# Group scores called ahead of the step's copies, 22 and 11 portions, the fourth MM1 block in a half tile, and two small VectorE operations in place of GpSimd's

## The chip, the cores and the metric

The kernel runs on one core of a Trainium2 chip. A core has five engines, each with an instruction queue of its own that it works off in order: TensorE (PE, with PEld for its weight loads), VectorE (DVE), ScalarE (ACT), GpSimd (POOL) and SyncE (SP, which here only issues transfers). Engines wait for one another through semaphores. The metric is the device time of one execution in microseconds.

## What is computed

Attention with one more term in the denominator, then a feed-forward layer with a Mish activation. The part that matters:

```python
q, k, v: (batch 8, heads 12, seq 448, head_dim 64), float32
w_in: (768, 2048), w_out: (2048, 768)

def _attn_ref(q, k, v):
    scores = scale * np.matmul(q, k.transpose(0, 1, 3, 2))
    m = np.max(scores, axis=-1, keepdims=True)
    e = np.exp(scores - m)
    attn = e / (np.sum(e, axis=-1, keepdims=True) + np.exp(-m) + 1e-09)
    return np.matmul(attn, v)

def _moe_ref(x, w_in, w_out):      # x: (batch * seq, heads * head_dim)
    h = x @ w_in
    sp = np.where(h > 20.0, h, np.log1p(np.exp(np.minimum(h, 20.0))))
    g = h * np.tanh(sp)
    return g @ w_out
```

## The kernel before

**Tiling.** Two heads make a pair, six pairs a batch (`HP`), 48 pairs in all. A pair takes four steps: in each, PE computes scores (L350 to L366) into a score tile, VectorE takes the negated row maxima (L369, `negm`), and ScalarE the exponentials with their sums (L387, into `en`). There are three score tiles in PSUM, `sc_tiles`, each of two halves of 512 float32 columns, used in turn: the scores of step i + 3 need the exponentials of step i done. Two single PSUM tiles, `mo_tiles`, serve everything else; they are handed out in the order in which they came back (`mo_take`, `mo_free`).

After a pair's last step VectorE forms the denominators and their reciprocals (`denominators`, L404 and L408). For most pairs of the first two batches the division comes later, as a multiplication of the outputs: the reciprocals are split into two bf16 parts, hi and lo (`hl`, L412 and L413), which PE spreads over the rows of a PSUM tile by 16 small matmuls (`spread_rden`, L432). The exponentials are transposed by a DMA (`normalise`, L462, `en` to `eT`), for a few pairs on PE (`turn_on_pe`). The product with v (`av_pair`, L497) follows some pairs later and gives `xT`.

**Units.** The first loop works on the six pairs 0 to 5 (`HEAD` is 6), the rest goes in units of three pairs, that is twelve steps (u from 2). After a unit's steps come eight blocks of the first matrix product (MM1: `mm1_mish`, `mm1`, six L556 matmuls each), each followed by ScalarE's Mish (L572) from PSUM into `gT`; blocks belong to the batch before. From u = 4 on the second product (MM2: `mm2_part`, L616, 16 matmuls for a portion of output columns) is spread over a unit's attention steps as a filler: a list of twelve weights says what share of it goes to which step. From u = 6 to 15 units are "grouped": the pairs' steps are mixed, the weights are `weight_paired`, and after steps 0, 2 and 4 no scores are written, so that two steps' scores come together after steps 1, 3 and 5 (`GROUP_AT`). Within a step the order of the calls is: exponentials, pending copies (`flush_late`), the filler's portions, scores.

**The order** of each engine's instructions is that of the calls: the program is scheduled by hand. Waits are put in by the framework, which follows what each instruction reads and writes tile by tile; where two instructions touch different halves of one tile, the code can declare them independent (`apart`, L237), and does so in attention at some places.

**Block banks.** `mm1_bank(ff, ahead)` puts the third block of a unit (index 2) into the first half of `sc_tiles[0]`, and if `ahead` is 2 the fourth block (index 3) into its second half; all others take a single tile. Before, `ahead` is 2 only for the blocks of the first batch (units 2 and 3), the first four of which in attention steps are begun early (`mm1_begin`).

**GpSimd's queue at the sixth pair.** In the first loop `load_w(n, behind=p-1)` makes GpSimd copy two elements of pair p-1's `eT` into `marks` (L172), which waits until that transfer has landed, then issue n weight transfers (L177); the reciprocals' parts and the casts of q, k and v (L194) stand behind these in its queue. The parts of pair 5, the sixth, are read by PE in unit 2, at step 5 (`RDEN_AT`).

Of the kernel before, what the change touches and what calls it, by code (L numbers as in the profile page):

```python
# [12 lines left out]
ALU = mybir.AluOpType  # L13
# [6 lines left out]
def kernel(  # L20
# [9 lines left out]
    nc = tc.nc  # L30
# [88 lines left out]
    def flush_late():  # L119
        while late:  # L120
            late.popleft()()
# [5 lines left out]
    def mo_take():  # L127

        if not mo_free:
            flush_late()  # L130
        return mo_free.popleft()
# [104 lines left out]
    def apart(later, *earlier):  # L236

        for e in earlier:
            tc.declare_no_dep(later.ins, e.ins, reason="they read different PSUM banks")
# [51 lines left out]
    def pair_step(idx):  # L291
        if idx < mixed_from:
            return divmod(idx, STEPS)
        u, at = divmod(idx, UNIT_PAIRS * STEPS)
        pi, s = MIXED[at]
        return u * UNIT_PAIRS + pi, s
# [24 lines left out]
    def scores_ahead(limit):  # L321

        n = max(0, min(limit - rg["next"], len(sc_tiles) - rg["used"]))
        for _ in range(n):
            rg["used"] += 1
            scores(rg["next"], paired=n > 1)
            rg["next"] += 1
# [48 lines left out]
    def exps(idx):  # L376
        p, s = pair_step(idx)
        if p >= N_PAIRS:
            return
        st = att[p]  # L380
        sc, cols = st.pop(("sc", s))
        rg["used"] -= 1
        if s == STEPS - 1 and p >= HP and p % UNIT_PAIRS == UNIT_PAIRS - 1:
            w = st["whole"]
            nc.scalar.activation(out=w["expm"], in_=w["negm"], func=AF.Exp)
        for bk, c in enumerate(cols):
            e = nc.scalar.activation(  # L387
                out=st["en"][:, :, c, 0:SP_],
                in_=sc[:, bk, 0:S].rearrange("q (j c) -> q j c", j=NT),
                func=AF.Exp, bias=st["negm"][:, c : c + 1], scale=1.0,  # L390
                accum_out=st["sums"][:, c : c + 1],
            )
            if idx in av_read:
                apart(e, av_read.pop(idx))
            if idx in av_beside:
                apart(e, *av_beside.pop(idx))
            if s == STEPS - 1:
                half_exp[p] = e
        if s == STEPS - 1 and p < HP:
            nc.scalar.activation(out=st["expm"], in_=st["negm"], func=AF.Exp)  # L400

    def denominators(p, n=1):
        st = att[p] if n == 1 else att[p]["whole"]
        nc.vector.scalar_tensor_tensor(  # L404
            out=st["den"], in0=st["sums"], scalar=1e-9, in1=st["expm"],
            op0=ALU.add, op1=ALU.add,
        )
        nc.vector.reciprocal(out=st["rden"], in_=st["den"])  # L408
        if p < LATE_DIV:
            hl = hl_pool.tile([128, 2, UNIT_PAIRS, NTILE], BF16, tag="hl", name="hl")  # L410
            hi, lo = (hl[:, x, 0, :] if n == 1 else hl[:, x, 0:n, :] for x in range(2))
            nc.gpsimd.tensor_copy(out=hi, in_=st["rden"])  # L412
            nc.gpsimd.tensor_tensor(out=lo, in0=st["rden"], in1=hi, op=ALU.subtract)  # L413
            for i in range(n):
                att[p + i]["hl"] = hl[:, :, i, :]

# [50 lines left out]
    def turn_on_pe(p, j, busy_first=0):  # L467

        st = att[p]
        own = mo_take()  # L470
        keep_busy(busy_first, bank=own)
        ps = own[:, :].bitcast(BF16).rearrange("c (i q) -> c i q", q=128)
        for i in range(NTILE):
            nc.tensor.transpose(ps[0:SP_, i, :], st["en"][:, j, i, 0:SP_], ident)

        def evac():
            nc.vector.tensor_copy(  # L477
                out=st["eT"][0:SP_, j, :].rearrange("c (i q) -> c i q", q=128),
                in_=ps[0:SP_, 0:NTILE, :],
            )  # L480
            mo_free.append(own)

        late.append(evac)
# [66 lines left out]
    def mm1_bank(ff, ahead=2):  # L550
        at = ff % FF_U - 2
        return sc_tiles[0][:, at, :] if 0 <= at < ahead else mo_take()

    def mm1(b, ff, bank, lo, hi):
        for dm in range(lo, hi):
            nc.tensor.matmul(  # L556
                bank[:, 0:S],
                lhsT=w_in_sb[:, dm, ff * 128 : (ff + 1) * 128],
                rhs=xT[b][:, dm, :],
                start=(dm == 0), stop=(dm == DM_T - 1),  # L560
            )

    def mm1_mish(b, ff):
        flush_late()
        at = ff % FF_U - 2
        spare = 0 <= at < (2 if b == 0 else 1)
        if (b, ff) in begun:
            h_ps, lo = begun.pop((b, ff))
        else:
            h_ps, lo = mm1_bank(ff, 2 if b == 0 else 1), 0  # L570
        mm1(b, ff, h_ps, lo, DM_T)
        nc.scalar.activation(out=gT[:, ff, b % 2 * S : b % 2 * S + S], in_=h_ps[:, 0:S], func=AF.Mish)  # L572
        if not spare:
            mo_free.append(h_ps)
# [79 lines left out]
    PAIRED_FROM = first_mm2 + 2  # L654
    GROUP_AT, AV_AT_STEP = (1, 3, 5), 8
    Q_AT = (0, 6, 7)
    weight_paired = [21, 0, 12, 0, 12, 0, 5, 6, 0, 0, 0, 0]

    LEAD = UNIT_PAIRS + 1
    LOAD_AT = (0, 3, 6)  # L660
# [1 line left out]
    HEAD = HP  # L662
# [26 lines left out]
    for p in range(HEAD):  # L689
        for s in range(STEPS):  # L690
# [11 lines left out]
            if s == 0:  # L702
                transpose_pair(p + 2)
                if p:
                    denominators(p - 1)
# [14 lines left out]
            if s < 3:  # L720
                keep_busy(2, half=p)
    denominators(HEAD - 1)

    for u in range(UNITS_PER_B, N_UNITS + 2 * UNITS_PER_B):
# [6 lines left out]
        grouped = attn and u >= PAIRED_FROM  # L731
# [5 lines left out]
        end = min(nxt, N_PAIRS) * STEPS  # L737

        for n in range(steps):
            defer[0] = attn and u > first_mm2 and nxt < N_PAIRS  # L740
            pi, s = divmod(n, STEPS)
            p, idx = p0 + pi, p0 * STEPS + n
            late_tp = u == UNITS_PER_B and n == STEPS
            exps(idx)
            if u == UNITS_PER_B + 1 and n == 0:
                for j in range(2):
                    turn_on_pe(HEAD, j, busy_first=3)
# [16 lines left out]
            if grouped and n == AV_AT_STEP:  # L764
# [1 line left out]
                    av_pair(p0 + i - UNIT_PAIRS, half=p0 + i)  # L766
                flush_late()
                av_pair(p0 - 1, act=True)
            if not grouped or n + 1 not in GROUP_AT:
                scores_ahead(end)  # L770
            if n in LOAD_AT and u <= first_mm2:
                at = p0 + LOAD_AT.index(n)
# [8 lines left out]
            elif n == 0 and u <= N_UNITS:  # L781
                nc.gpsimd.tensor_copy(  # L782
                    out=marks[0:1, 5, 0:2], in_=att[p0 - 1]["en"][0:1, NT - 1, NTILE - 1, 0:2]
# [12 lines left out]
            if (u, n) in MORE_LOADS:  # L796
                at = MORE_LOADS[u, n]
# [38 lines left out]
        b, w = (u - UNITS_PER_B) // UNITS_PER_B, u % UNITS_PER_B  # L836
# [3 lines left out]
        for f in range(FF_U):  # L840
            if moe:
                mm1_mish(b, w * FF_U + f)
            if u == UNITS_PER_B and f == 3:
                load_w(5, behind=p0 + 2)
            if u == first_mm2 - 1 and f == FF_U - 1:
                load_w(4, behind=p0 + 1)
            if not attn:
                continue
            if f == 0:
                denominators(p0, UNIT_PAIRS)  # L850
                for p in todo[:first]:
                    normalise(p, dma=p not in BY_PE)
            if f in (1, 3, 5):
                if nxt < BY_DMA_FROM:
                    transpose_pair(nxt + f // 2, bank=f // 2 % 2)
                    evac_qk(nxt + f // 2)
            if f == 1 and p0 < LATE_DIV:
                for p in todo[first:]:
                    normalise(p, dma=p not in BY_PE)
            if f == FF_U - 1:  # L860
                scores_ahead(min(nxt * STEPS + len(sc_tiles), N_PAIRS * STEPS))
            third = 5 if nxt >= BY_DMA_FROM else FF_U - 1
            if f in (3, third) and p0 >= LATE_DIV:
                p = todo[1 + f // 5]
                normalise(p, dma=p not in BY_PE)
# [32 lines left out]
```

## Time and profile before

| | us |
|---|---|
| median of three runs | 459.73 |
| lowest and highest | 454.26 and 459.82 |
| the profiled execution | 459.73 |
| its span in the profile | 457.9 |

| share of the span on the chain that ended last | |
|---|---|
| PE | 72% |
| ACT | 10% |
| DVE | 6% |
| issue (nothing that the profile shows was waited for) | 6% |
| DMA | 3% |
| POOL | 2% |

How to read the rows below. A row of a timeline is: start, length, engine, line of the kernel, operation, what it writes and reads, shapes, and the count, if several of the same kind run one after the other; in brackets how long the engine had been idle before, and what ended that. Matmuls overlap, so 0.36 us for one is its latency, and a row of many shows the rate. In a row of windows stand the window, its length, the busy times of PE, PEld, DVE, ACT and POOL with counts, the clock that TensorE was granted (1.00 is full), the mean busy share of the 16 DMA engines, and GB/s.

### The profile page before, as it was taken

The page shows a single profiled execution, that of the slowest core. Times are in us where ns is not written, and L with a number is a line of the kernel's source. Part 1 is how long each engine was busy: PE and PEld are TensorE (multiplying, and loading weights), DVE is VectorE, ACT ScalarE, POOL GpSimd, SP SyncE. Part 2 cuts the span into 40 slices and gives each one's busy share as a digit, 9 for nine tenths or more (in the row PEclk, how much of TensorE's full clock was granted, in tenths as well). Part 3 has the DMA queues.
Part 4 walks back from the last instruction along what each step waited for, and adds up shares of the span by engine and source line. Part 5 has one row for each costly group of instructions (what it writes and reads, how often), then busy time and mean ns, then how long its engine had stood idle before and what let it go on. Part 6 is the DMA issues. An engine that isn't in the chain of part 4 may idle for free.

```text
span 457.9 us, 8637 instructions
## 1 busy us (share of the span) xinstructions
PE 436.2 (95%) x2991; PEld 232.1 (51%) x2991; DVE 327.3 (71%) x666; ACT 335.8 (73%) x884; POOL 138.6 (30%) x269
## 2 busy tenths in 40 slices
PE   7878699999999999999999999999999999999996
PEld 3334355445555545545454545554554555556565
DVE  5999678888797868778787878786878878311021
ACT  5999578989787969798887979796979788221300
POOL 4442638316054233232424242413233210100000
PEclk9999899999999999999999999999999999999999
DMA  8999999999999999999999999999999793920213
GB/s 233 260 209 162 246 227 212 264 235 207 242 238 273 237 279 241 250 230 283 236 257 236 259 253 229 266 214 273 229 245 252 205 243 106 246 65 2 69 36 103
DMA packets 232652, 97.93 MB, mean 214 GB/s; under 512 B 189344, under 2 KB 229152, under 8 KB 232608
## 3 DMA queue, kind: packets, MB, share of 16 engines
q1 hardware_dynamic: 225088, 91.07, 86.9%
q0 software_dynamic: 7488, 6.29, 9.3%
q8 instruction: 23, 0.38, 0.4%
q14 instruction: 21, 0.17, 0.1%
q10 hardware_dynamic: 32, 0.01, 0.0%
HBM read 45.61 MB, written 11.01 MB: 124 GB/s over the span
## 4 chain that ended last, share of the span: by engine, by line
PE 72%; ACT 10%; DVE 6%; issue 6%; DMA 3%; POOL 2%; DVEq 0%; ACTq 0%; POOLq 0%
PE mo L556 27%; PE mo L616 24%; ACT en L387 7%; PE sc L497 5%; PE sc L356 4%; PE sc L556 4%; DVE negm L369 4%; DMA eT<-en 3%; PE sc L350 2%; PE mo L497 2%; ACT L387 2%; POOL w_in_sb L177 1%; DVE o_sb L601 1%; PE sc L309 1%; DVE eT L477 1%
## 5 line engine op out<-in xcount | busy, mean ns | idle before, releaser
L387 ACT ACTIVATE en<-sc,negm 128x448 bf16<-128x448 f32 x336 | 208.9, 640 | 12.4 <-DVE negm L369 11.7
L369 DVE TENSOR_REDUCE negm<-sc 128x2 f32<-128x896 f32 x192 | 179.4, 970 | 48.5 <-PE sc L359 36.1
L616 PE MATMUL mo<-w_out_sb,gT 128*128 128x384 bf16 (+1 forms) x1040 | 159.1, 304 | 0.0
L556 PE MATMUL mo<-xT,w_in_sb 128*128 128x448 bf16 x660 | 131.7, 353 | 0.9 <-DVE xT L517 0.3
L616 PEld LDWEIGHTS <-gT 128*128 128x128 bf16 x1040 | 93.9, 98 | 60.8 <-issue 13.9
L556 PEld LDWEIGHTS <-w_in_sb 128*128 128x128 bf16 x768 | 74.3, 98 | 70.9 <-issue 5.1
L572 ACT ACTIVATE gT<-mo 128x448 bf16<-128x448 f32 x110 | 58.3, 544 | 67.9 <-PE mo L556 67.7
L387 ACT ACTIVATION_READ_ACCUMULATOR en<-sc,negm 128x1 f32 x336 | 71.0, 211 | 0.0
L454 DVE TENSOR_SCALAR en<-en,rden 128x448 bf16<-128x448 bf16 x280 | 70.6, 331 | 0.6
L601 DVE COPY o_sb<-mo 128x192 f32<-128x192 f32 (+1 forms) x65 | 32.4, 498 | 50.2 <-PE mo L616 49.0
L273 POOL TENSOR_SCALAR qd<-qT_all 64x448 bf16<-64x448 bf16 x60 | 33.6, 560 | 89.2 <-DMA qT_all<-q_cast 49.3
L356 PE MATMUL sc<-kT_all,qd 64*128 64x448 bf16 x132 | 42.0, 363 | 2.7 <-ACT en L387 1.3
L359 PE MATMUL sc<-kT_all,qd 64*128 64x448 bf16 x132 | 42.5, 367 | 0.0
L782 POOL COPY marks<-en 1x2 bf16<-1x2 bf16 x12 | 2.1, 174 | 105.6 <-DVE en L454 105.6
L194 POOL CAST q_cast<-q_f 112x512 bf16<-112x512 f32 x47 | 28.9, 614 | 5.8 <-DMA q_f<-in_q_dram 5.8
L497 PEld LDWEIGHTS <-v_bf 112*64 112x64 bf16 x384 | 19.8, 110 | 20.8 <-issue 10.4
L497 PE MATMUL sc<-eT,v_bf 112*64 112x448 bf16 x256 | 29.2, 364 | 0.4 <-DMA eT<-en 0.4
L194 POOL CAST k_cast<-k_f 112x512 bf16<-112x512 f32 x47 | 28.8, 612 | 1.5 <-DMA k_f<-in_k_dram 1.4
L194 POOL CAST v_bf<-v_f 112x512 bf16<-112x512 f32 x48 | 28.2, 607 | 2.4 <-DMA v_f<-in_v_dram 2.4
L556 PE MATMUL sc<-xT,w_in_sb 128*128 128x448 bf16 x108 | 23.2, 353 | 0.0
L356 PEld LDWEIGHTS <-qd 64*128 64x128 bf16 x132 | 9.1, 95 | 26.7 <-issue 17.9
L350 PE MATMUL sc<-kT_all,qd 128*128 128x448 bf16 x60 | 19.2, 353 | 1.3 <-ACT en L387 1.1
(64 smaller groups left out, 267.8 us busy)
## 6 DMA issues: line engine op xcount, KB each, us to landing
k_f<-in_k_dram SPq DMA_DIRECT2D x48, 224.0 KB, 5.2
q_f<-in_q_dram SPq DMA_DIRECT2D x48, 224.0 KB, 5.3
v_f<-in_v_dram SPq DMA_DIRECT2D x48, 224.0 KB, 5.8
w_in_sb<-in_moe_w_in_dram POOLq DMA_DIRECT2D x12, 256.0 KB, 7.3
w_out_sb<-in_moe_w_out_dram POOLq DMA_DIRECT2D x8, 384.0 KB, 12.2
out_dram<-o_sb SPq DMA_DIRECT2D x7, 336.0 KB, 3.3
out_dram<-o_sb SPq DMA_DIRECT2D x8, 288.0 KB, 3.5
out_dram<-o_sb SPq DMA_DIRECT2D x8, 240.0 KB, 3.0
```

Of the source, the lines that this page charges most:

```text
L194: nc.gpsimd.tensor_copy(out=to[nm], in_=src)
L273: q_reads.append(by.tensor_scalar(out=qd[rows, h * S : (h + 1) * S], in0=q_ps[rows, 0:S], scalar1=SCALE, scalar2=1.0, op0=ALU.mult, op1=AL ...
L356: nc.tensor.matmul(sc[:, 0, 0:S], lhsT=qT[0:64, qa : qa + 128], rhs=kA, start=True, stop=True)
L359: nc.tensor.matmul(sc[:, 1, 0:S], lhsT=qT[64:128, qb : qb + 128], rhs=kB, start=True, stop=True)
L369: half_max[p] = nc.vector.tensor_reduce(out=negm, in_=sc[:, 0 : len(cols), 0:S], axis=AX.X, op=ALU.max, negate=True)
L387: e = nc.scalar.activation(out=st["en"][:, :, c, 0:SP_], in_=sc[:, bk, 0:S].rearrange("q (j c) -> q j c", j=NT), func=AF.Exp, bias=st["neg ...
L454: nc.vector.tensor_scalar(out=en[:, :, i, 0:SP_], in0=en[:, :, i, 0:SP_], scalar1=st["rden"][:, i : i + 1], scalar2=None, op0=ALU.mult,)
L497: mm = nc.tensor.matmul(av[h * 64 : (h + 1) * 64, 0:S], lhsT=v_bf[:, h, j * D : (j + 1) * D], rhs=e_h, start=(j == 0), stop=(j == NT - 1),)
L556: nc.tensor.matmul(bank[:, 0:S], lhsT=w_in_sb[:, dm, ff * 128 : (ff + 1) * 128], rhs=xT[b][:, dm, :], start=(dm == 0), stop=(dm == DM_T - 1),)
L572: nc.scalar.activation(out=gT[:, ff, b % 2 * S : b % 2 * S + S], in_=h_ps[:, 0:S], func=AF.Mish)
L601: nc.vector.tensor_copy(out=o_sb[:, cols], in_=st["o"][:, 0:n_cols])
L616: nc.tensor.matmul(st["o"][:, 0:n_cols], lhsT=gT[:, ff, i * 128 : (i + 1) * 128], rhs=w_out_sb[:, ff, cols], start=(ff == 0), stop=(ff == ...
```

## The change

Four edits. The hi and lo parts of the sixth pair's reciprocals are made by VectorE instead of GpSimd. The fourth MM1 block goes into the second half of the first score tile in all batches, not only in the first. The weights of steps 0 and 2 in grouped units are 22 and 11 instead of 21 and 12; their sum stays 56. In grouped units the scores of steps 1, 3 and 5 are called right after the exponentials, ahead of pending copies and the filler's portions.

```diff
@@ -409,8 +409,9 @@
         if p < LATE_DIV:
             hl = hl_pool.tile([128, 2, UNIT_PAIRS, NTILE], BF16, tag="hl", name="hl")
             hi, lo = (hl[:, x, 0, :] if n == 1 else hl[:, x, 0:n, :] for x in range(2))
-            nc.gpsimd.tensor_copy(out=hi, in_=st["rden"])
-            nc.gpsimd.tensor_tensor(out=lo, in0=st["rden"], in1=hi, op=ALU.subtract)
+            by = nc.vector if p == HEAD - 1 else nc.gpsimd
+            by.tensor_copy(out=hi, in_=st["rden"])
+            by.tensor_tensor(out=lo, in0=st["rden"], in1=hi, op=ALU.subtract)
@@ -563,11 +564,11 @@
     def mm1_mish(b, ff):
         flush_late()
         at = ff % FF_U - 2
-        spare = 0 <= at < (2 if b == 0 else 1)
+        spare = 0 <= at < 2
         if (b, ff) in begun:
             h_ps, lo = begun.pop((b, ff))
         else:
-            h_ps, lo = mm1_bank(ff, 2 if b == 0 else 1), 0
+            h_ps, lo = mm1_bank(ff), 0
@@ -654,7 +655,7 @@
-    weight_paired = [21, 0, 12, 0, 12, 0, 5, 6, 0, 0, 0, 0]
+    weight_paired = [22, 0, 11, 0, 12, 0, 5, 6, 0, 0, 0, 0]
@@ -742,6 +743,8 @@
             exps(idx)
+            if grouped and n in GROUP_AT:
+                scores_ahead(end)
             if u == UNITS_PER_B + 1 and n == 0:
@@ -766,7 +769,7 @@
-            if not grouped or n + 1 not in GROUP_AT:
+            if not grouped or (n not in GROUP_AT and n + 1 not in GROUP_AT):
                 scores_ahead(end)
```

## The prediction

> **What bounds the kernel now.** I read the page first, then the busy time by windows, then the order of events at the three places that the diff touches.
>
> ```profile
> span 457.9 us, 8637 instructions
> ## 1 busy us (share of the span) xinstructions
> PE 436.2 (95%) x2991; PEld 232.1 (51%) x2991; DVE 327.3 (71%) x666; ACT 335.8 (73%) x884; POOL 138.6 (30%) x269
> ```
> ```profile
> 40.00:80.00 40.00, 34.56 (x332) 19.59 (x333) 30.77 (x58) 30.62 (x83) 22.47 (x42) 0.96 1.17 225
> 54.70:58.10 3.40, 3.40 (x21) 1.27 (x18) 1.41 (x2) 1.77 (x5) 3.40 (x7) 0.50 1.23 206
> 200.00:250.00 50.00, 49.65 (x318) 25.67 (x318) 39.95 (x83) 42.01 (x111) 17.01 (x32) 1.00 1.10 247
> ```
>
> In the steady part (200 to 250 us; the columns are length, then busy time of PE, PEld, DVE, ACT and POOL, granted clock, DMA share, GB/s) PE works 49.65 of 50.00 us at full clock. PE takes its instructions in order, so whatever makes it wait there adds to the time, unless a later wait shrinks by as much. From 40 to 80 us PE is busy for 34.56 of 40.00 us only, the mean clock is 0.96 and the DMA share 1.17: that stretch has slack on PE and none on the transfers. The profiled run took 459.73 us, 1.83 us more than its span; it is also the median of the three runs, so I add to 457.9 and put 1.83 us on top.
>
> **Part 1, the fourth MM1 block in a half tile.** In units 4 to 17 (14 of them, one per unit) the six matmuls of the fourth block go to the second half of the first score tile instead of one of the two single tiles. The instructions, their number and their order stay. What changes is what the first of them waits for. Here is that place in one grouped unit (PE's L556, ScalarE's Mish L572).
>
> ```profile
> 163.47 1.30 PE L556 MATMUL sc<-xT,w_in_sb 128*128 128x448 bf16 x6
> ...
> 164.20 0.98 ACT L572 ACTIVATE gT<-mo 128x448 bf16<-128x448 f32 x2
> 164.80 1.67 PE L556 MATMUL mo<-xT,w_in_sb 128*128 128x448 bf16 x8
> ...
> 165.06 0.55 ACT L572 ACTIVATE gT<-sc 128x448 bf16<-128x448 f32 x1
> ```
>
> The third block (into the half tile) starts at 163.47, and the fourth at 164.80. Eight matmuls in 1.67 us, the last of 0.36 (the length that single matmuls show at 199.53 below), are one per 0.187 us, so PE was free at 163.47 + 6 x 0.187 = 164.59 and waited 0.21 us. It waited for the first block's Mish, which gives its tile back: the two Mish from 164.20 take 0.98, one is 0.54 long, so the first ends at 164.74 and the matmul starts 0.06 later. After the change no single tile has to come free. But a wait is kept by whole tiles, the third block's Mish reads the first half of the very tile whose second half the fourth block writes, and the code declares no independence between the two. The waits of the changed program, which can be read without running it, say so: in all 14 units the first matmul of block four waits for the ScalarE count that the Mish of the third block brings. That Mish runs from 165.06 to 165.61; the fourth block starts at 165.67 instead of 164.80: +0.87 us for each of ten grouped units. Behind it on PE stand all later blocks and the next unit's scores, and ScalarE's later Mish wait for those, so nothing takes it up. The four other units:
>
> ```profile
> 113.91 0.54 PE L556 MATMUL mo<-xT,w_in_sb 128*128 128x448 bf16 x2
> 114.11 0.54 ACT L572 ACTIVATE gT<-sc 128x448 bf16<-128x448 f32 x1
> ...
> 427.68 1.11 PE L556 MATMUL mo<-xT,w_in_sb 128*128 128x448 bf16 x5
> ...
> 427.94 0.54 ACT L572 ACTIVATE gT<-sc 128x448 bf16<-128x448 f32 x1 [0.60 <-PE sc L556]
> ```
>
> The first pair (unit 4) gives 114.11 + 0.54 + 0.06 - 113.91 = 0.80, taken for units 4 and 5; the second (unit 17) 0.86, taken for 16 and 17. Sum of part 1: 8.7 + 1.6 + 1.7 = **+12.0 us**. The old wait lies inside the difference. If the wait had no effect on the chip, the part would be worth -0.21 x 10 = -2.1 us: its other bound.
>
> The Trainium skill ("PSUM — Partial Sum Buffer", The four PSUM rules) says that each PSUM bank is a memory of its own and that one matmul's output fits one bank. By it, a half of this tile is a bank, and PE could fill one while ScalarE reads the other, so the chip does not need this wait; by it part 1 would be the -2.1 us. The trace of before shows no such overlap at this place, and the program's wait decides.
>
> **Part 2, portions 22 and 11.** In each of the ten grouped units one L616 matmul moves from behind the first group of scores to ahead of it.
>
> ```profile
> 199.53 0.36 PE L356 MATMUL sc<-kT_all,qd 64*128 64x448 bf16 x1
> ...
> 199.98 0.35 PE L356 MATMUL sc<-kT_all,qd 64*128 64x448 bf16 x1
> ...
> 202.34 0.36 PE L359 MATMUL sc<-kT_all,qd 64*128 64x448 bf16 x1
> 202.53 0.35 PE L356 MATMUL sc<-kT_all,qd 64*128 64x448 bf16 x1
> 202.54 0.35 PE L359 MATMUL sc<-kT_all,qd 64*128 64x448 bf16 x1
> 202.82 2.12 PE L616 MATMUL mo<-w_out_sb,gT 128*128 128x384 bf16 x12
> ...
> 207.87 0.35 PE L350 MATMUL sc<-kT_all,qd 128*128 128x448 bf16 x1
> ```
>
> From the scores at 199.53 a chain runs: VectorE's maximum, the exponentials, the next scores in the same tile (202.53), the twelve portions at 202.82, scores, maximum, exponentials, and the scores at 207.87. It is 8.34 us long and the portions of the weight that shrinks (12 to 11) lie beside its exponentials, so one fewer there only makes PE wait. Ahead of 199.53 PE works without a gap, and one more portion there moves the start of the chain by (2.12 - 0.33) / 11 = 0.163 us (twelve in 2.12, the last of them 0.33, an estimate from the 0.35 of its neighbours). Ten units: **+1.6 us**. The scores behind, at 199.98, come 0.45 us after the first, where those at 202.53 follow those at 202.34 after 0.19, so they wait 0.26 themselves; were it that wait which counts, the portion would fill it, and the part be worth -1.6. I take the chain, since its steps follow each other without a gap.
>
> **Part 3, the sixth pair's bf16 parts on VectorE.** Before, GpSimd's queue holds them up, and PE with them:
>
> ```profile
> 50.45 0.36 PE L359 MATMUL sc<-kT_all,qd 64*128 64x448 bf16 x1
> 54.02 1.00 PE L432 MATMUL mo<-ident,hl 128*64 128x128 bf16 x16 [3.21 <-POOL hl L412]
> 54.95 1.71 PE L497 MATMUL sc<-eT,v_bf 112*64 112x448 bf16 x8
> ...
> 60.08 0.95 PE L497 MATMUL sc<-eT,v_bf 112*64 112x448 bf16 x8
> ```
> ```profile
> 50.74 0.17 POOL L172 COPY marks<-eT 1x2 bf16<-1x2 bf16 x1 [3.66 <-DMA eT<-en]
> 50.86 2.90 POOL L177 DMA_DIRECT2D w_in_sb<-in_moe_w_in_dram  x4
> 53.74 0.23 POOL L412 CAST hl<-rden 128x7 bf16<-128x7 f32 x1
> ```
> ```profile
> 42.74 0.16 DVE L404 SCALAR_TENSOR_TENSOR den<-sums,expm 128x7 f32<-128x7 f32 x1
> 43.00 0.20 DVE L408 RECIPROCAL rden<-den 128x7 f32<-128x7 f32 x1
> ```
>
> GpSimd waits for a transposed tile until 50.74, issues four weight transfers (2.90 us) and only then makes the part; PE stands 3.21 us, and for 3.40 us after that its clock is 0.50 (second row of the windows). The eight L497 matmuls cost 1.71 instead of the 0.95 they cost at 60.08, so the clock costs 0.76 at least and half of 3.40 = 1.7 at most; I take 1.1. On VectorE the two operations stand right behind the reciprocal and ahead of the next maximum; the nearest rows (0.16, 0.20, started 0.26 apart) put them at 0.3 to 0.5, I take 0.45, and they delay that maximum once. The L497 that follows needs the tile that had landed at 50.74, so it is ready. The gain at this place is 3.2 + 1.1 - 0.45 = **3.9 us**. GpSimd is rid of 0.4 us, and its weight transfers and casts stay behind the same tile: nothing is added.
>
> Does it reach the end? The transfers of that stretch are full (1.17 in the windows), and two later waits go by them:
>
> ```profile
> 69.50 0.17 POOL L172 COPY marks<-eT 1x2 bf16<-1x2 bf16 x1 [6.29 <-DMA eT<-en]
> ```
> ```profile
> 108.55 0.76 PE L497 MATMUL sc<-eT,v_bf 112*64 112x448 bf16 x6 [0.42 <-DMA eT<-en]
> ```
>
> GpSimd waits 6.29 us for a transposed tile before its next weights, and at 108.55 PE itself waits 0.42 us for one: there is no slack at that point, so only as much of the 3.9 is kept as the transfers come earlier. The bounds are 0 and -3.9; with neither row nearer I take half, **-2.0 us**.
>
> **Part 4, scores called ahead of the step's copies**, moves no instruction: at steps 1, 3 and 5 no copy is pending, and each engine's order there is the same as before. Zero; nothing is there to be hidden.
>
> **Sum.** +12.0 + 1.6 - 2.0 = +11.6: a span of 469.5 and a time of **471.3 us** (+2.5%).
>
> **Rivals.** *B, the other side:* the fourth block starts without the wait for the third Mish, because the two halves do not disturb each other. Then part 1 is -2.1, and the sum -2.1 + 1.6 - 2.0 = -2.5: 457.2 us. Its place is the gap at 164.59; it decides from the point where the fourth block starts less than 0.03 us later per unit than now (the 0.4 us that parts 2 and 3 leave, over 14 units). For it: ScalarE has read the first half when it is done at 165.61, PE needs only the second. Against it: the wait stands in the program. *C, the gain of part 3 is kept whole:* 471.3 - 1.9 = 469.4. For it: a tile is issued when VectorE has made it, so it is issued 3.9 earlier; against: the 0.42 at 108.55. *D, the transfers keep all of it:* 473.3. The transposed tiles would then be issued earlier, into weight transfers that are still under way.
>
> The Trainium skill ("DMA: Bandwidth & Descriptors", Queues, rings and completion order) says that each DMA engine goes round the queue rows that have work, one packet at a time. By it an earlier transposed tile shares the engines with the weights instead of waiting behind them, and part of the shift is kept, which is between C and D; the share above 1 in the windows fits several queues at work, but no row here separates them.
>
> *E, the portion fills the wait at 199.98:* part 2 is -1.6 instead of +1.6, 468.1. *The change does less than it says:* part 4 is that already, at no cost either way.
>
> **Numbers.** Chances: forecast 0.55, B 0.07, C 0.15, D 0.13, E 0.10. A measurement here tells about 2%, that is, below 450.5 or above 468.9. E and B lie within, C half a microsecond beyond the edge, forecast and D beyond it. Faster by over 2% needs a cause that I don't see: 0.02. Within: B, E and about a third of C and a sixth of the rest, 0.27. Slower: 0.71. The range reaches from C and E together (471.3 - 1.9 - 3.2 = 466.2), with 0.5 for the clock's bound, to D with part 3's VectorE work charged at the next pairs as well and 0.1 more lag per unit (473.3 + 0.3 + 1.4): 465.7 to 475.0; B and a small rest are left out.
>
> **What would show it.** In the changed profile, per grouped unit: block four starts behind the end of the third Mish, a PE gap near 1.1 us there (0.21 + 0.87) put down to ScalarE's L572, and a unit longer by some 1.0 us; PE busy in the steady window down from 49.65 to about 47.9 of 50 (0.87 less for each of the two units in it). L432 starts at about 51 without a gap, and no slice has the clock at 0.50 there; the wait of PE for a transposed tile (0.42 before) grows to some 2 us. Wrong would be a fourth block that overlaps the third Mish (B), or a unit that is longer by less than 0.8 us (E).

## The result and the profile after

The changed kernel takes 473.25 us (median of 6 runs, 471.07 to 480.31), the kernel before 459.03 us (6 runs beside it): a ratio of 1.031, interval 1.025 to 1.038. The execution of 480.31 us was a slow one, and the ratio is taken without it. The profiled execution took 473.83 us, its span is 472.1 us, 14.2 more than before. The page of the changed kernel, beginning and the two rows of 40 slices that matter:

```profile
span 472.1 us, 8638 instructions
## 1 busy us (share of the span) xinstructions
PE 435.7 (92%) x2991; PEld 232.6 (49%) x2991; DVE 325.6 (69%) x668; ACT 335.4 (71%) x884; POOL 138.4 (29%) x267
...
PE   6878999979999999999989899999999898999997
...
PEclk9999999979999999999999999999999999999999
```

PE does the same work (435.7 us against 436.2) in a longer span: the time has gone into waits. PE's own list of waits in the changed kernel (what waited, for what: total, times, longest) names them:

```profile
PE sc L557 <- ACT gT L573: 12.0, 14, 1.0
PE sc L350 <- ACT en L387: 3.6, 12, 0.3
PE sc L498 <- DMA eT<-en: 3.2, 1, 3.2
```

The first row is the fourth MM1 block, once in each of 14 units. Its place in the timeline, first grouped unit (the same place as in the prediction; L557 is L556 of before, L573 is L572):

```profile
165.70 1.30 PE L557 MATMUL sc<-xT,w_in_sb 128*128 128x448 bf16 x6
166.44 0.98 ACT L573 ACTIVATE gT<-mo 128x448 bf16<-128x448 f32 x2
167.30 0.55 ACT L573 ACTIVATE gT<-sc 128x448 bf16<-128x448 f32 x1
167.90 0.92 PE L557 MATMUL sc<-xT,w_in_sb 128*128 128x448 bf16 x4 [0.91 <-ACT gT L573]
```

The third Mish ends at 167.85 and the fourth block starts at 167.90. From the third block's start to the fourth's it is 2.20 us, where it was 1.33: +0.87. The 0.91 in brackets counts from the modelled end of the last matmul; by the rate of 0.187 us per matmul PE stands 2.20 - 6 x 0.187 = 1.08 us.

The chain of the grouped units in PE's timeline, with one portion less between the first group's scores and the next:

```profile
203.83 0.36 PE L356 MATMUL sc<-kT_all,qd 64*128 64x448 bf16 x1
...
204.12 0.35 PE L356 MATMUL sc<-kT_all,qd 64*128 64x448 bf16 x1
...
204.42 1.96 PE L617 MATMUL mo<-w_out_sb,gT 128*128 128x384 bf16 x11
206.31 0.36 PE L356 MATMUL sc<-kT_all,qd 64*128 64x448 bf16 x1
...
206.83 0.35 PE L356 MATMUL sc<-kT_all,qd 64*128 64x448 bf16 x1
...
212.18 0.35 PE L350 MATMUL sc<-kT_all,qd 128*128 128x448 bf16 x1 [0.30 <-ACT en L387]
```

From 203.83 to 212.18 it is 8.35 us: the chain kept its length (8.34), and the place of the portion that was taken out is a gap (206.83 follows 206.31 after 0.52, where it was 0.19). Of the 0.33 that it grew, one half is that portion; the other comes from the scores at 204.12, which follow the first after 0.29 now, where it was 0.45. The portion did shorten that wait, as rival E says, but the wait isn't on the chain. The 0.30 ahead of the last scores is the second row of the list of waits, once in each grouped unit and twice elsewhere.

The sixth pair's parts, and what became of them, in the timelines of VectorE, PE and GpSimd:

```profile
43.33 0.17 DVE L413 CAST hl<-rden 128x7 bf16<-128x7 f32 x1
43.54 0.17 DVE L414 TENSOR_TENSOR hl<-rden,hl 128x7 bf16<-128x7 f32 x1
```
```profile
51.26 0.70 PE L433 MATMUL mo<-ident,hl 128*64 128x128 bf16 x16
...
96.95 1.71 PE L498 MATMUL sc<-eT,v_bf 112*64 112x448 bf16 x8 [3.15 <-DMA eT<-en]
```
```profile
47.20 0.18 POOL L172 COPY marks<-eT 1x2 bf16<-1x2 bf16 x1 [1.67 <-DMA eT<-en]
47.33 2.88 POOL L177 DMA_DIRECT2D w_in_sb<-in_moe_w_in_dram  x4
```
```profile
98.00:102.00 4.00, 4.00 (x15) 1.51 (x12) 2.28 (x3) 0.29 (x1) 1.66 (x3) 0.50 1.10 250
```

PE doesn't wait for the parts any more. But GpSimd's mark stands at 47.20 here, not at 50.74: the transposed tile came 3.5 us earlier in this execution than in the profiled one of before. No edit of the diff brings that: its transfer was issued at the same time (36.81 and 36.79) and took 10.33 us instead of 13.90, and runs 1 and 3 below have the early tile without part 3. And PE waits 3.15 us at 96.95 instead, for another transposed tile, with the clock at 0.50 behind that wait (last row, a window).

Put side by side, the starts of the same instruction in the two timelines show where the 14.2 us arise (the 336 exponentials of L387 are numbered in the order in which they start):

| instruction | before | after | after - before |
|---|---|---|---|
| exponential number 64 (unit 3) | 71.59 | 67.09 | -4.50 |
| number 85 (unit 4) | 96.55 | 92.06 | -4.49 |
| number 99 (unit 4, behind the wait at 96.95) | 106.20 | 106.83 | +0.64 |
| number 106 (unit 5, behind unit 4's blocks) | 122.43 | 123.70 | +1.27 |
| number 127 (unit 6) | 147.75 | 149.83 | +2.07 |
| number 148 (unit 7) | 172.52 | 175.63 | +3.11 |
| number 316 (unit 15) | 370.76 | 382.15 | +11.39 |
| fourth block's Mish in unit 17 | 429.07 | 443.20 | +14.12 |

Each grouped unit adds 1.035 us ((11.39 - 3.11) / 8), of which 0.87 lie at the fourth block and 0.165 at the portion. Number 99 to number 106 holds two things. From the third block's start to the fourth's it is 1.13 us longer in unit 4; and the wait of 0.42 us at 108.55, which the profile of before has there, is missing in this execution. The runs that have neither the new wait nor that old one (3, 6, 9 and 11) gain 0.49 between the two numbers, and 1.13 - 0.49 is the 0.64 of the table.

### The profile page after: what moved, and what is told of

Read it like the earlier page. It is cut to its first block, busy times and chain, and to the rows that moved or that the text cites. A ratio compares the mean times of both kernels' runs of the same rounds, so it can differ in the third digit from the quotient of the medians.

```text
span 472.1 us, 8638 instructions
## 1 busy us (share of the span) xinstructions
PE 435.7 (92%) x2991; PEld 232.6 (49%) x2991; DVE 325.6 (69%) x668; ACT 335.4 (71%) x884; POOL 138.4 (29%) x267
## 4 chain that ended last, share of the span: by engine, by line
PE 59%; ACT 15%; DVE 11%; issue 3%; DMA 2%; DVEq 0%; ACTq 0%
PE mo L617 22%; PE mo L557 17%; DVE negm L369 9%; ACT en L387 8%; PE sc L557 5%; PE sc L498 5%; PE sc L356 4%; ACT gT L573 4%; ACT L573 3%; DMA eT<-en 2%; PE sc L350 2%; PE mo L498 2%; DVE eT L478 1%; ACT expm L385 0%; PE mo L309 0%
## 5 line engine op out<-in xcount | busy, mean ns | idle before, releaser
L387 ACT ACTIVATE en<-sc,negm 128x448 bf16<-128x448 f32 x336 | 209.1, 640 | 18.8 <-DVE negm L369 17.7
L557 PE MATMUL mo<-xT,w_in_sb 128*128 128x448 bf16 x576 | 115.2, 352 | 0.6 <-ACT gT L573 0.3
L557 PEld LDWEIGHTS <-w_in_sb 128*128 128x128 bf16 x768 | 74.2, 98 | 82.9 <-issue 17.2
L573 ACT ACTIVATE gT<-mo 128x448 bf16<-128x448 f32 x96 | 50.7, 545 | 59.9 <-PE mo L557 59.8
L387 ACT ACTIVATION_READ_ACCUMULATOR en<-sc,negm 128x1 f32 x336 | 70.9, 211 | 0.0
L557 PE MATMUL sc<-xT,w_in_sb 128*128 128x448 bf16 x192 | 41.4, 352 | 12.0 <-ACT gT L573 12.0
L356 PE MATMUL sc<-kT_all,qd 64*128 64x448 bf16 x132 | 40.6, 361 | 3.3 <-ACT en L387 2.3
L359 PE MATMUL sc<-kT_all,qd 64*128 64x448 bf16 x132 | 41.0, 364 | 0.0
L573 ACT ACTIVATE gT<-sc 128x448 bf16<-128x448 f32 x32 | 17.3, 551 | 21.2 <-PE sc L557 21.2
```

What stands on the lines that cost most here:

```text
L356: nc.tensor.matmul(sc[:, 0, 0:S], lhsT=qT[0:64, qa : qa + 128], rhs=kA, start=True, stop=True)
L359: nc.tensor.matmul(sc[:, 1, 0:S], lhsT=qT[64:128, qb : qb + 128], rhs=kB, start=True, stop=True)
L387: e = nc.scalar.activation(out=st["en"][:, :, c, 0:SP_], in_=sc[:, bk, 0:S].rearrange("q (j c) -> q j c", j=NT), func=AF.Exp, bias=st["neg ...
L557: nc.tensor.matmul(bank[:, 0:S], lhsT=w_in_sb[:, dm, ff * 128 : (ff + 1) * 128], rhs=xT[b][:, dm, :], start=(dm == 0), stop=(dm == DM_T - 1),)
```

## The experiments

All ratios are against runs of the kernel before on the same chip, with their intervals. Offsets are starts of the same exponential against the profile of before, as in the table.

**1. Part 1 alone.**

```diff
-        spare = 0 <= at < (2 if b == 0 else 1)
+        spare = 0 <= at < 2
-            h_ps, lo = mm1_bank(ff, 2 if b == 0 else 1), 0
+            h_ps, lo = mm1_bank(ff), 0
```

> The kernel before with part 1 alone: the fourth MM1 block in the second half of the first score tile in all batches. Theory (the new wait for the third block's Mish sets the time): the fourth block starts 0.8 to 0.87 us later in each of units 4 to 17, 11.8 us in all as the changed kernel's offsets show, span 457.9 + 11.8 = 469.7, ratio 1.026. Rival (the 0.87 comes from the parts together, the portion and the half tile): less than 6 us, ratio under 1.013.

Ratio 1.032 (1.027 to 1.036), span 468.9. The same row of waits, to the digit:

```profile
PE sc L556 <- ACT gT L572: 12.0, 14, 1.0
```

From unit 6 to unit 15 the offset grows by 0.87 per unit. This part carries the slowdown. The execution shows a second thing, in PE's timeline, though GpSimd makes the sixth pair's parts here as it did before:

```profile
51.01 0.36 PE L359 MATMUL sc<-kT_all,qd 64*128 64x448 bf16 x1
51.30 0.70 PE L432 MATMUL mo<-ident,hl 128*64 128x128 bf16 x16
```

There is no wait for GpSimd: its second part was done at 51.09, in time. At number 64 this run leads the profile of before by 4.45 us, without part 3.

**2. Part 3 alone.**

```diff
-            nc.gpsimd.tensor_copy(out=hi, in_=st["rden"])
-            nc.gpsimd.tensor_tensor(out=lo, in0=st["rden"], in1=hi, op=ALU.subtract)
+            by = nc.vector if p == HEAD - 1 else nc.gpsimd
+            by.tensor_copy(out=hi, in_=st["rden"])
+            by.tensor_tensor(out=lo, in0=st["rden"], in1=hi, op=ALU.subtract)
```

> The kernel before with part 3 alone: VectorE makes the sixth pair's bf16 parts. Theory (the transfers take all of it back and the cold clock is paid again at the later wait): 4.5 us ahead until unit 4, then a wait of some 3.2 us for a transposed tile and a clock of 0.50 behind it, at the end +0.6 us, span 458.5. The prediction's value: -2.0, span 455.9. Rival C: -3.9, span 454.0.

Ratio 1.001 (0.997 to 1.005): no gain, and -3.9 us (0.991) is excluded, -2.0 (0.996) just so. In the one profile the lead is 3.2 us at unit 3 and 2.65 at the end (span 455.3), not the wait of 3.2 us that was expected: near 97 us PE doesn't wait for a tile here, and at 105.87 it waits 0.9 us for the next one. So neither value describes every execution: the stretch up to 110 us differs between executions of the same program.

**3. Part 2 alone.**

```diff
-    weight_paired = [21, 0, 12, 0, 12, 0, 5, 6, 0, 0, 0, 0]
+    weight_paired = [22, 0, 11, 0, 12, 0, 5, 6, 0, 0, 0, 0]
```

> The kernel before with part 2 alone, weights 22 and 11. Theory: each of the ten grouped units is 0.16 us longer, +1.6 us, span 459.5. Rival E (the portion fills a wait): -1.6, span 456.3.

Ratio 1.008 (1.005 to 1.011), span 458.2; the offset grows by 1.66 us over the ten grouped units (from -1.37 to +0.29), 0.165 each. The direction and the size in the units are as forecast, rival E is out. The ratio stands for 2.2 to 4.9 us, more than the units show; the program is the same as before up to unit 6, so the rest would have to come from the first 110 us of these 4 runs, and that isn't settled.

**4. The changed kernel without the new wait.** Fourth block's matmuls and third block's Mish are declared independent, since they use different halves (abridged):

```diff
+        mms = mm1(b, ff, h_ps, lo, DM_T)
+        if b and at == 1:
+            for mm in mms:
+                apart(mm, blk3[0])
...
+        elif at == 1 and b:
+            apart(m, *blk3[1])
```

> The changed kernel with the fourth block's matmuls declared independent of the third block's Mish, since the two use different halves of the tile. Theory: the wait of 0.86 us at the fourth block is gone in 14 units, and the 0.21 us that were there before too: 472.1 - 11.8 - 2.1 = 458.2 us of span, ratio 1.00. Rival (the chip itself makes PE wait where ScalarE reads the other half, or the stall only moves to the fifth block): span above 465.

Ratio 1.003 (1.000 to 1.006). The timeline of PE at the two blocks:

```profile
160.13 2.43 PE L560 MATMUL sc<-xT,w_in_sb 128*128 128x448 bf16 x12
```

Third and fourth block run as one row of twelve without a gap, while the first two Mish are still at work. The third block's Mish starts at 161.73, and the fourth block's matmuls run from 161.26 to 162.56, so the two overlap in the two halves. Undoing the wait alone takes away the slowdown; the chip didn't make PE wait at the other half.

**5. The fourth block in the half tile, declared independent, and nothing else**, and **6. the fourth block in another score tile, without a declaration** (the diff is run 6's, abridged; unit 4 keeps its single tile there):

```diff
     def mm1_bank(ff, ahead=2, apart_by=0):
         at = ff % FF_U - 2
+        if apart_by and at == 1 < ahead:
+            return sc_tiles[1][:, 0, :]
```

> The kernel before with the fourth block in the half tile and its matmuls declared independent of the third block's Mish; nothing else of the change. Theory: the fourth block starts as soon as PE is free, 0.2 us earlier in each of the ten grouped units than before, -2.1 us, ratio 0.995. Rival: the wait only moves on to the next block, ratio 1.00 with a PE wait of 0.2 us at the fifth block.

> The kernel before with the fourth block in the first half of the second score tile, which the third block's Mish does not read, in units 5 to 17, without any declaration (unit 4 keeps its single tile). Theory (it is the shared tile that makes the wait): no wait, as in the run above, -2 us, ratio 0.995 to 1.00. Rival (any bank off the single tiles costs the 0.87 us): ratio 1.025.

5: ratio 0.998 (0.995 to 1.001); 6: 0.997 (0.993 to 1.001). In both the offset falls by 0.18 to 0.19 us per grouped unit (run 6: +0.66 at unit 6, -1.01 at unit 15), the old wait of 0.2. So it is the shared tile that made the new wait, not the use of a score tile. Whether the kernel is faster as a whole isn't shown: -1.7 us lies inside both intervals. Run 5 had the wait for GpSimd of its own accord, in PE's timeline:

```profile
54.52 0.93 PE L432 MATMUL mo<-ident,hl 128*64 128x128 bf16 x16 [2.26 <-POOL hl L412]
```

**7 and 8. GpSimd made late at the sixth pair**, without and with part 3:

```diff
             n_marks[0] += 1
+            if behind == HEAD - 2:
+                for _ in range(6):
+                    nc.gpsimd.tensor_copy(out=gT[:, FF_T - 1, S : 2 * S], in_=busy)
```

> The kernel before with six copies of 128x448 more on GpSimd in front of the marks of the sixth pair, some 3.4 us: the late GpSimd of the profiled execution of before, made on purpose. Theory (the stall was one execution's, and the transfers decide at the end): L432 of the sixth pair waits about 3 us for GpSimd again and the clock falls to 0.50 behind it, and of these 4 us at most 1.5 are left at the end, ratio 1.000 to 1.004. Rival (the stall costs in full): +4 us, ratio 1.009.

> The same six copies, with part 3 of the change. Theory: no wait at L432, time as without the copies, ratio 0.997 to 1.003. If the stall costs in full, this is 4 us faster than the run before it.

Ratios 1.003 (1.000 to 1.006) and 1.000 (0.997 to 1.003). Run 7 missed its condition: the six copies took 3.67 us, but from 45.13 to 48.75, mostly while the mark would have waited for its tile anyway, and L432 waited 0.29 us only. The pair says nothing on the question, and the copies were moved:

**9 and 10. The parts held up in every execution**, without and with part 3:

```diff
+            if p == HEAD - 1:
+                for _ in range(6):
+                    nc.gpsimd.tensor_copy(out=gT[:, FF_T - 1, S : 2 * S], in_=busy)
             nc.gpsimd.tensor_copy(out=hi, in_=st["rden"])
```

> The kernel before with six copies of 128x448 more on GpSimd (3.67 us in the earlier run) straight in front of the sixth pair's bf16 parts, so that they are late in every execution. Theory: L432 of that pair waits 3 to 3.6 us for GpSimd and the clock falls behind it, the lead at the scores of unit 3 is some 4 us smaller than in runs without the wait, and the wait for the transposed tile near 97 us is smaller by 1 to 3 us, so that 0 to 2 us are left at the end: ratio 1.000 to 1.004. Rival (the stall reaches the end in full): ratio 1.009.

> The same six copies at the same place with part 3 of the change, so that only GpSimd's casts behind them are late. Theory: no wait at L432, ratio 0.997 to 1.003. If the stall reaches the end in full, 4 us faster than the run before it.

Run 9: ratio 1.009 (1.006 to 1.013), its L432:

```profile
54.77 1.27 PE L435 MATMUL mo<-ident,hl 128*64 128x128 bf16 x16 [4.10 <-POOL hl L415]
55.97 1.71 PE L500 MATMUL sc<-eT,v_bf 112*64 112x448 bf16 x8
```

A wait of 4.10 us and the cold 1.71 us behind it, as in the profile of before. Run 10: 1.001 (0.998 to 1.004), no wait. My theory of that moment (0 to 2 us left at the end) falls. By the medians the stall costs 0.8% or 3.8 us, with an error of some 2; in the two profiles run 9 is 1.08 us ahead of run 10 at exponential 43, 4.60 behind at number 64, 3.50 at number 106 and 2.87 at number 127: the stall costs 5.7 us at its place, and 3.95 of them are left. So most of it is kept, and a part is won back where run 9 does not wait for a transposed tile and run 10 does (1.8 us in three waits).

**11. Half the rows of the first four w_out transfers left out.**

```diff
-                    w_out_sb[:, f : f + 4, h * c_out : (h + 1) * c_out],
-                    moe_w_out[f * 128 : (f + 4) * 128, h * c_out : (h + 1) * c_out],
+                    w_out_sb[:, f : f + (4 if h else 2), h * c_out : (h + 1) * c_out],
+                    moe_w_out[f * 128 : (f + (4 if h else 2)) * 128, h * c_out : (h + 1) * c_out],
```

> The kernel before with half the rows left out of the first four w_out transfers, the left-out rows set to zero by GpSimd in a stretch where it idles; those rows of the second product are not computed. Theory (the transfers of 70 to 93 us set when the transposed tile of 85 to 90 us lands): that tile lands 3 us or more earlier after its issue (6 us instead of 7.4 to 11.3), PE's wait near 97 us is gone, ratio 0.990 to 0.995. Rival (the tile's own transfer is slow, whatever else is under way): the wait stays, ratio 1.00.

Ratio 0.997 (0.994 to 1.000), less than expected. PE has no wait for a transposed tile near 97 us; that alone shows little, as the profiles of before and of runs 2, 9 and 12, with all the weights, have none there either. What differs is the time to landing. The window before it, run 11 and then the changed kernel, and the DMA view of 84 to 92 us of both (q0 is the queue of the weights: packets, MB, share of 16 engines; then the tiles issued there, two in run 11, with the median time to landing):

```profile
85.00:93.00 8.00, 7.72 (x62) 4.36 (x60) 6.36 (x23) 6.82 (x15) 0.52 (x2) 1.00 0.82 201
q0 software_dynamic: 9, 0.01, 0.5%
eT<-en SPq DMA_TRANSPOSE x2, 5.1
```
```profile
85.00:93.00 8.00, 7.93 (x52) 4.24 (x52) 7.11 (x19) 6.82 (x15) 0.00 (x0) 1.00 1.33 207
q0 software_dynamic: 763, 0.56, 44.9%
eT<-en SPq DMA_TRANSPOSE x1, 11.3
```

With the weights out of the way and the DMA share at 0.82 the tile lands in 5.1 us, with 1.33 in 11.3. The record of all profiles says more. In the thirteen with all the weights this tile landed 3.25 to 3.40 us after the last of the q, k and v loads that SyncE had issued ahead of it in its own queue, no matter when it was issued itself (from 85.50 in run 8 to 91.11 in run 9); in the changed kernel that load landed at 93.64 and the tile at 96.91. In run 11 the load was through at 88.76, 0.67 us after the tile was issued. That load itself took 12.3 us from issue to landing in the changed kernel and 7.1 in run 11. By these numbers the tile stands in line behind SyncE's own loads, and what the weights slow down is these. This execution had a wait of 1.6 us for GpSimd at the sixth pair, another one that came by itself.

**12. The other tile, with weights 20 and 13.**

```diff
-    weight_paired = [21, 0, 12, 0, 12, 0, 5, 6, 0, 0, 0, 0]
+    weight_paired = [20, 0, 13, 0, 12, 0, 5, 6, 0, 0, 0, 0]
```

> The kernel with the fourth block in the second score tile, as in the earlier run, and the weights 20 and 13 instead of 21 and 12. Theory: the fourth block's 0.2 us are gained in ten units as there; one portion less ahead of the chain of 8.34 us lets it start 0.16 us earlier, but the chain's next scores then come behind one portion more, so 0 to -1.6 us beside it: ratio 0.992 to 0.997. Rival (the portion only moves the wait): as the run with 21 and 12, 0.997, or above.

Ratio 1.002 (0.999 to 1.006): no gain on 21 and 12. In the profile the offset falls by 0.06 us per grouped unit instead of the 0.18 to 0.19 of run 6, so this way costs 0.12. The two ends of the chain in PE's timeline:

```profile
194.92 0.36 PE L356 MATMUL sc<-kT_all,qd 64*128 64x448 bf16 x1
...
203.58 0.35 PE L350 MATMUL sc<-kT_all,qd 128*128 128x448 bf16 x1
```

It has 8.66 us now instead of 8.34: thirteen portions no longer fit beside the exponentials. No version tried is shown to be faster than the kernel before.

## Why the prediction came out as it did

**Part 1** (+12.0 forecast): right, with its mechanism. From the third block's start to the fourth's it is 0.87 us longer in each grouped unit, 1.13 in unit 4 (0.80 was taken), 0.79 in unit 5 and 0.86 in units 16 and 17, in all 12.3. Unit 4 was taken too low because there the wait of 0.42 us at 108.55 is missing after the change: PE reaches the block earlier against ScalarE, and so waits longer for its Mish (the third block starts 1.64 us ahead of its Mish, where it was 1.34). Runs 1, 4 and 6 show the mechanism from three sides: alone it costs as much as the whole change, without the wait the cost is gone, and in a tile that the Mish doesn't read there is no wait. What was taken from the Trainium skill ("PSUM — Partial Sum Buffer", The four PSUM rules), that the chip doesn't need this wait, agrees with run 4: there PE fills one half while ScalarE reads the other. What cost the time was the program's wait, which is kept by whole tiles. Rival B was the kernel that the edit could have been.

**Part 2** (+1.6): right, 1.65 over ten units, and the chain of 8.34 us was the right reason. Run 12 adds that 21 and 12 is the balance: a portion more on either side of the first group costs 0.12 to 0.165 us per unit.

**Part 3** (-2.0): this term failed; it came out at about +0.1 in the profile (14.1 less 12.3 and 1.65), and at nothing that run 2 can measure. The step that failed is "The gain at this place is 3.2 + 1.1 - 0.45 = 3.9 us". Its prices were off by less than a microsecond. Between numbers 43 and 64 the lead over the profile of before grows by 5.02 us in runs 1, 3 and 6, where GpSimd made the parts in time, and by 4.53 in the changed kernel and in runs 2, 8 and 10, where VectorE made them: the stall was worth 5.0 us, so 1.8 of it the clock, about the upper bound of 1.7 and not 1.1, and VectorE's two operations cost 0.5 (0.45 was taken). But the wait of 3.21 us was taken for a feature of the program, and it was one of the profiled execution: among the seven profiles in which GpSimd makes the parts without copies being added (before, runs 1, 3, 5, 6, 11, 12) it is 3.21, 0, 0, 2.26, 0, 1.62 and 0. It goes by when the tile of the pair before lands, since GpSimd's mark waits for it; where that was between 46.1 and 48.8 us the parts were in time, at 50.2 to 51.2 they weren't. The row said so: GpSimd's 50.74 was released by a DMA after 3.66 us. Where there is no stall, part 3 only costs VectorE's 0.5 us at this place.

The second step of part 3, that half is kept since the transfers decide later, is nearer: of the stall's 5.7 us, run 9 against run 10 leaves 3.95 in the profiles, and the medians say 3.8, with an error of some 2, so it is rather two thirds. That PE would wait for a transposed tile was right, 3.15 us instead of the "some 2 us" forecast, but it is another tile than the one of 108.55, and the clock of 0.50 behind it was not in the sum: from number 85 to number 99 the kernel loses 5.1 us, 2.0 more than the wait itself. That the earlier tile meets weight transfers still under way is what rival D said. The Trainium skill ("DMA: Bandwidth & Descriptors", Queues, rings and completion order) would have transfers of different queues share the engines packet by packet; the 11.3 us under a share of 1.33 against 5.1 us under 0.82 agree with that. The 3.25 to 3.40 us behind SyncE's last load, in thirteen profiles, show that the tile also stands in line in its own queue.

**Part 4** (zero): right as far as the record goes. It was not run alone, but PE's 2991 matmuls stand in the same order in the profile of run 3, which lacks part 4, as in that of the changed kernel, and the 0.87 of run 1 and the 0.165 of run 3 make up the whole 1.035 us of a grouped unit.

The sum was 11.6 us for the span and 14.2 were measured: of the 2.6 between them 2.1 are part 3 and 0.3 unit 4's block. Rival D's 473.3 is the measured time. In the profiled execution its reason holds too, as the whole lead of 4.5 us is lost by number 99; as a rule it doesn't, by runs 9 and 10. One figure of the working doesn't follow from its own terms: B, E, a third of C and a sixth of the rest add up to 0.33, not 0.27, for a time within 2%.

## What to carry to other kernels

When a buffer is moved to a free half of a tile, ask what the framework tracks: if waits are kept by whole tiles, the neighbour's reader becomes a new wait, and it shows in the program before anything runs; a tile of its own or a declared independence takes it away. A wait in one profile that ends with a transfer's landing may belong to that execution: look whether a second profile has it before its length goes into a sum. In a pipeline that is balanced to a tenth of a microsecond, moving one piece of filler in either direction costs about its own length per round.

## What the runs showed of the hardware

Behind PE's stalls of 3.21 us (before, until 54.02), 3.15 us (the changed kernel, until 96.95) and 4.10 us (run 9, until 54.77) the clock was 0.50, and eight matmuls that take 0.95 us at full clock took 1.71. It stayed at 0.50 for 3.4 us in the first and for some 5.4 (97.0 to 102.4) and 4.3 in the others. The length of the stall alone doesn't decide: behind 2.21 us in run 1 (until 96.06) and 2.00 us in run 3 (until 96.43) the clock was 0.50 too, from 96.5 to 99.8 and from 97.3 to 100.6, and behind the 2.26 us of run 5 at 54.52 and its 2.05 us at 99.34 it was 1.00.

The time from issue to landing of one and the same transposed tile (issued at 85 to 91 us) ran from 5.6 to 11.3 us among the profiles with all the weights, and PE's wait near 97 us from 0 to 3.2 us. How much of the scatter between runs of one kernel comes from that isn't shown, as each kernel has one profile.
